# An attention backward kernel: dV and dK accumulated transposed, with 512 moving columns, and turned back on TensorE

## The chip, the cores and the metric

The kernel runs on one core of a Trainium2 chip. The metric is the device time of one execution in microseconds. Three runs of the kernel before gave 5147.52, 5152.12 and 5171.49 us, median 5152.12. Engines are called PE (TensorE: matmuls, and its weight loads PEld), DVE (VectorE), ACT (ScalarE), POOL (GpSimd) and SP (SyncE, which here issues transfers).

## The reference

Forward, with x of 2048 x 576 in bf16:

```
xn = layernorm(x)
s  = attention(xn @ wq, k_cache, v_cache) @ wo      # 32 heads, 2048 keys, 128 wide
g  = silu( (sigmoid(xn@w_gate) * (xn@w_up)) @ w_down )
out = x + s * g
```

The kernel returns `out` and the gradients with respect to x, both caches, wq, wo and the three weights of the gated block. For one head, with Q, K, V, dO of 2048 x 128, the attention part is

```
P  = softmax(Q K^T * 128**-0.5)      dV = P^T dO
dP = dO V^T                          dS = P * (dP - delta),  delta = rowsum(O * dO)
O  = P V                             dQ = dS K      dK = dS^T Q   (dQ, dK times the scale)
```

## The kernel before

Three stages surround each other: the gated block forward (to about 516 us), the 32 heads (to about 3767 us) and the weight gradients with dx (to the end). Only the heads are changed.

**Tiles of a head.** Queries go in 16 tiles of 128 rows (`qt`). For each, the scores of 2048 keys are made in two halves of 1024 columns (`s_half`: two matmuls of 512 moving columns into one of the two buffers of `ps_big`). DVE scales each half, takes the running minimum and writes `sneg`; ACT makes the exponential of the whole row (`s_exp`) into a slab `Pq` of 128 x 2048. P is left unnormalized; one over the row sum (`rinv`) is multiplied into dO's natural form `dOn` on POOL, two tiles at a time (`s_scale`), and into the outputs. In the same manner `dp_half` makes dP in two halves. The first half is usually moved out by ACT as `t` (minus delta) and multiplied by P on DVE; the second is one DVE instruction. The results are slabs `dSq`. There are 20 slabs for P and dS together.

**Two kinds of products.** The row passes (`row_mm`, L525) make O and dQ. They need P and dS transposed, which SP's transposing transfers give (`PT`, `dST`, one tile of dS by PE). Four query tiles share one accumulator bank. The column passes (`kv_mm`, L544) make dV and dK and use the slabs as they are: a block of 128 slab columns is the stationary operand, `dOn` or `Qn` of the same query tile moves with 128 columns, and the sum over the 16 query tiles stands in PSUM as [keys, 128]. A pass covers half of the keys, that is 8 blocks in two banks, 128 matmuls. When the last query tile is done, `sink` copies each bank to a staging tile `kv` (ACT) and POOL issues its output.

**The natural and transposed forms.** `prep_kt`, `prep_vt`, `prep_don` and `prep_qn` each turn eight 128 x 128 blocks on PE into one bank (`pt`, name `acct`), and one copy of 128 x 1024 moves it to SBUF. `proj` (L424, L425) makes Q^T and dO^T in four chunks of 512 columns.

**Banks.** `ps_acc` has four PSUM banks for everything but scores and dP: row accumulators, column accumulators (two per pass), projections and all transposes. `wt` has two buffers per tag; `t` is one tag.

**The order.** It is written out by hand. Every step gets a position with `at(pos, ...)`; a head has 64 positions (`HEAD`), S halves stand at 0 to 31 and dP halves at 32 to 63 (`anchor`), and the next head begins at 64, so that dK's passes and the last rows of dQ lie in the S half of the next head. The list is sorted by position and issued in that order, and under `manual_schedule` PE, DVE and ACT execute in this very order. In steady heads one position lasts about 1.57 us. SP's and POOL's instructions are ordered by a planner; they too run in order on their queues. The positions that matter here:

```
VA, VB, KA, KB = (22, 38.0), (38.5, 53.5), (58.0, 69.5), (70.5, 82.0)
QP, DO, KVE, PJE, OUE = (41.0, 3.0), (4.0, 2.5), "ss", "sv", "s"
KT_AT, DON_AT, VT_AT, QN_AT = (46.3, 2, "v"), (7.2, 5, "v"), (22.2, 2, "v"), (38.3, 2, "s")
EXP_AT, RINV_AT, PT_AT, DST_AT, AFTER = 2.1, 4.6, 2.7, 2.0, 3.5
```

VA and VB are start and end of dV's two passes (first and second half of the keys), KA and KB those of dK's; positions over 64 are in the next head (82 is its 18). The `_AT` triples are the position of the first group of eight blocks, the step to the second, and the engine of the copy, "v" DVE or "s" ACT. The exponential of tile qt stands at 2 qt + 2.1.

Of the kernel before, what the change touches and what calls it, by code (L numbers as in the profile page):

```python
# [9 lines left out]
bf = mybir.dt.bfloat16  # L10
f32 = mybir.dt.float32
PSUM = bass.MemoryType.PSUM
DRAM = bass.MemoryType.DRAM
P = 128
# [81 lines left out]
def kernel(  # L96
# [6 lines left out]
    nc = tc.nc  # L103
# [6 lines left out]
    NT = S // P  # L110
# [4 lines left out]
    CH = min(512, S)  # L115
# [32 lines left out]
    ident = pers.tile([P, P], bf, name="ident")  # L148
# [5 lines left out]
    alt = Alt(nc)  # L154
# [22 lines left out]
    with tc.tile_pool(name="pa", bufs=1) as pa:  # L177
        wd_sb = pa.tile([P, FT, D], bf, name="wd_sb")
        with tc.tile_pool(name="a1w", bufs=1) as wp:
# [11 lines left out]
            for bi in range(len(bounds) - 1):  # L191
                c0, c1 = bounds[bi], bounds[bi + 1]
# [72 lines left out]
        if True:  # L265
# [9 lines left out]
            with tc.tile_pool(name="a2h", bufs=1, reuse_waits="tile") as hp, \  # L275
# [12 lines left out]
                for sg in range(NT // SG):  # L288
# [7 lines left out]
                    for sl in range(SG):  # L296
# [7 lines left out]
                        for ft in range(FT):  # L304
                            for j, (n0, nn) in enumerate(ncs):
                                nc.tensor.matmul(accs[j][:, :nn], lhsT=hT_st[:, ft, :], rhs=wd_sb[:, ft, n0:n0 + nn],  # L306
                                                 start=(ft == 0), stop=(ft == FT - 1))
# [25 lines left out]
    KPC = CH // P  # L333
# [4 lines left out]
    with tc.tile_pool(name="ld2", bufs=2) as ld2, tc.tile_pool(name="ld1q", bufs=1) as ld1q, \  # L338
# [17 lines left out]
        def at(pos, fn, *args):  # L356
            prog.append((pos, len(prog), fn, args))

        def anchor(pos, fn, *args):
            anchors.append((pos, len(anchors), fn, args))  # L360
# [175 lines left out]
            if after:  # L536
                at(pos + step * (GQ - 1) + width + AFTER, after)

        def kv_mm(bx, hs, slabs, rhs, half, qt, j, sink):
            i, jj = j // KPC, j % KPC  # L540
            if qt == 0 and jj == 0:
                bx.acc[i] = ps_acc.tile([P, KPC, P], f32, name="acckv", tag="acc")
            k0 = (half * 2 * KPC + j) * P
            nc.tensor.matmul(bx.acc[i][:, jj, :], lhsT=slabs[qt][:, k0:k0 + P], rhs=getattr(hs, rhs)[:, qt, :],  # L544
                             start=(qt == 0 and jj == 0), stop=(qt == NT - 1 and jj == KPC - 1))
            if qt == NT - 1 and jj == KPC - 1:
                sink(bx.acc[i], i)

        def kv(pos, end, hs, slabs, rhs, half, out_dram):
            ov = out_dram.rearrange("(p t) d -> p t d", t=NT)  # L550
            bx = Box()
            bx.acc = [None, None]

            def sink(acc, i):
                c = half * 2 + i
                kv_t = stg.tile([P, KPC, P], bf, name="kv")
                alt.copy(kv_t[:], acc[:], eng=KVE[i])
                nc.gpsimd.dma_start(ov[:, c * KPC:(c + 1) * KPC, :], kv_t[:])

            n = 2 * KPC  # L560
            for qt in range(NT):
                for j in range(n):
                    at(pos + (end - pos) * (qt * n + j) / (NT * n), kv_mm, bx, hs, slabs, rhs, half, qt, j, sink)

        def o_sink(hs, g):
            gs = slice(g * GQ, (g + 1) * GQ)
# [28 lines left out]
        H1 = 2 * NT  # L595
        HEAD = 2 * H1
        XO, XQ = 12.1, 12.1
        VA, VB, KA, KB = (22, 38.0), (38.5, 53.5), (58.0, 69.5), (70.5, 82.0)
        QP, DO, KVE, PJE, OUE = (41.0, 3.0), (4.0, 2.5), "ss", "sv", "s"
        KT_AT, DON_AT, VT_AT, QN_AT = (46.3, 2, "v"), (7.2, 5, "v"), (22.2, 2, "v"), (38.3, 2, "s")  # L600
        EXP_AT, RINV_AT, PT_AT, DST_AT, AFTER = 2.1, 4.6, 2.7, 2.0, 3.5
        WO_AT = 50.0
        MAN = {mybir.EngineType.PE, mybir.EngineType.DVE, mybir.EngineType.Activation}
        for h in range(H):
            hs = Head(h)
            b = h * HEAD
            back = lambda x: b - HEAD + x if h else b - 14 + x / 8
            at(back(35.0), load_w, hs)
            at(back(35.1), load_kv, hs)
            for c in range(NCH):  # L610
                at(back(QP[0] + QP[1] * c), proj, hs, "QT", c, PJE[0])
                at(b + DO[0] + DO[1] * c, proj, hs, "dOT", c, PJE[1])
            at(b + DO[0] - 2, prep_wo, hs, "s")
            for g in range(2):
                at(back(KT_AT[0] + KT_AT[1] * g), prep_kt, hs, g, KT_AT[2])
                at(b + DON_AT[0] + DON_AT[1] * g, prep_don, hs, g, DON_AT[2])
                at(b + VT_AT[0] + VT_AT[1] * g, prep_vt, hs, g, VT_AT[2])
                at(b + QN_AT[0] + QN_AT[1] * g, prep_qn, hs, g, QN_AT[2])
            for p in range(NT // 2):
                at(b + 4 * p + 2 + RINV_AT, s_rinv, hs, p)  # L620
                at(b + max(4 * p + 2.1 + RINV_AT, DON_AT[0] + DON_AT[1] * (p // 4) + 0.5), s_scale, hs, p)
            for qt in range(NT):
                p1, p2 = b + 2 * qt, b + H1 + 2 * qt
                for hf in range(NHF):
                    anchor(p1 + hf, s_half, hs, qt, hf)
                    anchor(p2 + hf, dp_half, hs, qt, hf)
                at(p1 + EXP_AT, s_exp, hs, qt)
                if qt in PE_P:
                    for g in range(2):
                        at(p1 + 5.3 + g, trans_pe, hs.PT, hs.P, qt, "PT", g, "s")  # L630
                else:
                    at(p1 + PT_AT, trans_dma, hs.PT, hs.P, qt, "PT")
                if qt in PE_DS:
                    for g in range(2):
                        at(p2 + 4.3 + g, trans_pe, hs.dST, hs.dS, qt, "dST", g, "sv"[g])
                else:
                    at(p2 + DST_AT, trans_dma, hs.dST, hs.dS, qt, "dST")
            for g in range(NG):
                rows(b + 8 * g + XO, 2, 2, hs, hs.PT, "Vn", g, o_sink(hs, g))
                rows(b + H1 + 8 * g + XQ, 2, 2, hs, hs.dST, "Kn", g, dq_sink(hs, g))  # L640
            for half, (pv, pk_) in enumerate(((VA, KA), (VB, KB))):
                kv(b + pv[0], b + pv[1], hs, hs.P, "dOn", half, out_3[0, h])
                kv(b + pk_[0], b + pk_[1], hs, hs.dS, "Qn", half, out_2[0, h])
        bl = (H - 1) * HEAD
        assert WX + WD + 1 >= H
        for k, (h0, h1) in enumerate(((0, 8), (8, 16), (16, WX), (WX, WX + 7), (WX + 7, WX + WD))):
            if h0 < H - 1:
                at(bl + WO_AT + 3 * k, load_wo, h0, min(h1, H - 1))
        prog.sort(key=lambda e: e[:2])
# [10 lines left out]
    if True:  # L660
# [16 lines left out]
        with tc.tile_pool(name="c1b", bufs=1, side="right", reuse_waits="tile") as blk, \  # L677
# [32 lines left out]
            for st in range(NT):  # L710
# [12 lines left out]
                for h in range(H):  # L723
                    for j, (n0, nn) in enumerate(ncs):
                        nc.tensor.matmul(accs[j][:, :nn], lhsT=oT[:, h, :], rhs=wo_view(h)[:, n0:n0 + nn],
                                         start=(h == 0), stop=(h == H - 1))
# [17 lines left out]
        with tc.tile_pool(name="b1o", bufs=2, reuse_waits="tile") as outp, tc.tile_pool(name="b1t", bufs=3, reuse_waits="tile") as tmpp, \  # L744
# [21 lines left out]
            for fb in range(F // FB):  # L766
# [61 lines left out]
                for fl in range(FB // P):  # L828
                    frows = slice(fb * FB + fl * P, fb * FB + (fl + 1) * P)
                    accs = [ps.tile([P, 512], f32, name=f"accd{j}", tag="b") for j in range(len(ncs))]  # L830
                    for st in range(NT):
                        for j, (n0, nn) in enumerate(ncs):
                            nc.tensor.matmul(accs[j][:, :nn], lhsT=h_blk[:, st, fl * P:(fl + 1) * P], rhs=doB[:, st, n0:n0 + nn],  # L833
                                             start=(st == 0), stop=(st == NT - 1))
# [10 lines left out]
                for i in range(DL):  # L845
                    acc = ps.tile([P, 512], f32, name="accw", tag="b")
                    for st in range(NT):
                        nc.tensor.matmul(acc[:], lhsT=xn_all[:, st, i * P:(i + 1) * P], rhs=dd_blk[:, st, :, :],  # L848
                                         start=(st == 0), stop=(st == NT - 1))
                    alt.copy(stg_[:, i, :, :], acc[:].rearrange("p (k f) -> p k f", k=2))  # L850
                acc = ps.tile([P, 512], f32, name="accw", tag="b")
                for st in range(NT):
                    for k in range(2):
                        nc.tensor.matmul(acc[k * KL:(k + 1) * KL, :FB], lhsT=xn_all[:, st, DL * P:], rhs=dd_blk[:, st, k, :],
                                         start=(st == 0), stop=(st == NT - 1))
# [13 lines left out]
        with tc.tile_pool(name="c2b", bufs=1, reuse_waits="tile") as blk, tc.tile_pool(name="c2s", bufs=2, reuse_waits="tile") as sb, \  # L869
# [25 lines left out]
            for hg in range(NHG):  # L895
                cols = slice(hg * HG * P, (hg + 1) * HG * P)
                onb, dqb = held.pop(hg)
                for hl in range(HG):
                    h = hg * HG + hl
                    accs = [ps.tile([P, 512], f32, name=f"acc{j}") for j in range(len(ncs))]  # L900
                    for st in range(NT):
                        for j, (n0, nn) in enumerate(ncs):
                            nc.tensor.matmul(accs[j][:, :nn], lhsT=onb[:, st, hl * P:(hl + 1) * P], rhs=ds_all[:, st, n0:n0 + nn],  # L903
                                             start=(st == 0), stop=(st == NT - 1))
# [30 lines left out]
        with tc.tile_pool(name="c4c", bufs=1, reuse_waits="tile") as chp, tc.tile_pool(name="c4s", bufs=2, reuse_waits="tile") as sb, \  # L935
# [10 lines left out]
            for sbi in range(S // SB2):  # L946
# [7 lines left out]
                for pi, (src_d, wT, k0, KC, nm) in enumerate(passes):  # L954
# [5 lines left out]
                    for kk, sl in ([(kk, sl) for sl in range(nsl) for kk in range(KC)] if last else  # L960
# [3 lines left out]
                        for j, (n0, nn) in enumerate(ncs):  # L964
                            nc.tensor.matmul(accs[sl][j][:, :nn], lhsT=ch[:, kk, sl * P:(sl + 1) * P], rhs=w_[:, n0:n0 + nn],  # L965
                                             start=(pi == 0 and kk == 0), stop=(last and kk == KC - 1))
                for sl in range(nsl):
# [17 lines left out]
                    t = sb.tile([P, D], f32, name="t")  # L985
# [38 lines left out]
```

## Time and profile before

| | |
|---|---|
| median of three runs | 5152.12 us |
| profiled execution, its own time | 5157.5 us |
| its span | 5155.7 us |
| first exponential of head 0, last dQ copy of head 31 | 512.8, 3767.7 us |
| granted TensorE clock | 0.994 of full over the span, 1.00 in the heads |
| PE, DVE, ACT, POOL busy over the span | 97%, 63%, 44%, 27% |
| the same in head 20 (2530.60 to 2630.90 us) | 98.05, 84.53, 59.56, 32.73 of 100.30 us |
| a sneg half on DVE (L467) | 1.28 or 1.22 us |
| an exponential on ACT (L476) | 2.00 us |
| a copy of one bank, 512 f32 columns: ACT, DVE | 0.587, 0.689 us |
| a copy of one bank, 1024 bf16 columns: ACT, DVE | 1.018, 0.690 us |
| an output of dV or dK (L558): x256, issue on POOL, to landing | 0.553, 5.2 us |

A line of the groups names the line of the program, the engine, the operation, out<-in with buffer numbers left out, the shapes, the count, busy time and mean duration, and then the idle time before these instructions and what ended it. A line of the timeline has start, length, engine, line and operation; neighbours of one kind are merged, with their count, and in brackets stands an idle time before and what released it. Matmuls are pipelined, so the length of one is not what a further one costs: that is read from the distance of starts. A matmul of 128 moving columns is written 128x128, one of 512 columns 128x512.

### The profile page before, as it was taken

Reading aid. Unit: us, or ns where it says so; the run is one execution under the profiler, and the core shown is the slowest. Engines: PE = TensorE matmul, PEld = TensorE weight load, DVE = VectorE, ACT = ScalarE, POOL = GpSimd, SP = SyncE. Lnnn points to the kernel's source line nnn. Section 1 sums busy time; section 2 is a strip of 40 time slices with the busy share of each in tenths; the row PEclk is TensorE's granted clock in tenths of the full one; section 3 lists DMA queues with packets and bytes.
Section 4 is the critical chain, followed back from the end, with each engine's and each line's share of the span. In section 5 each row is a group of like instructions: output and inputs, shape, how many; then the busy total and the mean of one; then the engine's idle time right before and its main releaser. Section 6 shows DMA issues by size and latency. Waiting matters only on the chain.

```text
span 5155.7 us, 124622 instructions
## 1 busy us (share of the span) xinstructions
PE 4983.8 (97%) x53232; PEld 3490.9 (68%) x54160; DVE 3231.5 (63%) x5070; ACT 2285.3 (44%) x2878; POOL 1388.1 (27%) x1981
## 2 busy tenths in 40 slices
PE   8999999999999999999999999999899999999999
PEld 3444777777777777777777777777655555554554
DVE  5545888888888888888888888888733222210101
ACT  6531665566556556655655665566501222100000
POOL 2222333233223323332332333233222222111000
PEclk9999999999999999999999999999999999999999
DMA  7478999999999999999999999999999776697775
GB/s 281 184 210 166 189 191 196 195 199 195 196 196 196 197 201 199 196 202 196 199 196 198 199 197 195 199 199 195 205 200 246 209 209 196 199 246 166 158 153 118
DMA packets 2710509, 1013.89 MB, mean 197 GB/s; under 512 B 2523360, under 2 KB 2643936, under 8 KB 2709952
## 3 DMA queue, kind: packets, MB, share of 16 engines
q1 hardware_dynamic: 2628256, 726.57, 81.9%
q0 software_dynamic: 81696, 279.29, 18.5%
q8 instruction: 423, 6.93, 0.5%
q14 instruction: 134, 1.10, 0.1%
HBM read 172.54 MB, written 201.00 MB: 72 GB/s over the span
## 4 chain that ended last, share of the span: by engine, by line
PE 84%; DVE 6%; DMA 5%; issue 4%; SPq 1%; ACT 0%; DVEq 0%; ACTq 0%; another core or an unknown queue 0%
PE acckv L544 17%; PE acc L525 14%; PE acc L965 8%; PE dp L495 6%; PE sp L465 5%; DVE sneg L467 5%; PE accp L424 5%; PE accw L848 5%; DMA dST<-dSq 3%; PE g_ps L249 3%; PE u_ps L252 3%; PE accd L833 3%; PE acc L306 3%; PE acc L903 2%; PE dh L782 2%
## 5 line engine op out<-in xcount | busy, mean ns | idle before, releaser
L476 ACT ACTIVATE Pq<-sneg,nm 128x2048 bf16<-128x2048 bf16 x512 | 1024.5, 2001 | 389.5 <-DVE sneg L467 386.4
L525 PE MATMUL acc<-Kn,dST 128*128 128x128 bf16 x8192 | 1066.6, 219 | 28.1 <-DMA dST<-dSq 26.1
L544 PE MATMUL acckv<-dOn,Pq 128*128 128x128 bf16 x8192 | 1032.1, 219 | 15.4 <-POOL negdelta L579 0.2
L525 PE MATMUL acc<-Vn,PT 128*128 128x128 bf16 x8192 | 1023.2, 219 | 10.9 <-DMA PT<-Pq 9.1
L498 DVE SCALAR_TENSOR_TENSOR dSq<-dp,delta,Pq 128x1024 bf16<-128x1024 f32 x608 | 773.9, 1281 | 351.6 <-PE dp L495 249.7
L544 PE MATMUL acckv<-Qn,dSq 128*128 128x128 bf16 x8192 | 897.7, 220 | 8.4 <-issue 0.2
L544 PEld LDWEIGHTS <-Pq 128*128 128x128 bf16 x8192 | 793.8, 98 | 117.6 <-issue 0.9
L525 PEld LDWEIGHTS <-dST 128*128 128x128 bf16 x8192 | 758.8, 98 | 162.9 <-DMA dST<-dSq 34.1
L525 PEld LDWEIGHTS <-PT 128*128 128x128 bf16 x8192 | 766.4, 98 | 151.2 <-DMA PT<-Pq 11.3
L544 PEld LDWEIGHTS <-dSq 128*128 128x128 bf16 x8192 | 719.7, 98 | 99.8 <-issue 0.3
L467 DVE TENSOR_SCALAR_CACHE_REDUCE sneg<-sp,nm 128x1024 bf16<-128x1024 f32 x512 | 656.5, 1282 | 83.8 <-PE sp L465 46.4
L467 DVE TENSOR_SCALAR_CACHE_REDUCE sneg<-sp 128x1024 bf16<-128x1024 f32 x512 | 625.1, 1221 | 60.4 <-PE sp L465 42.0
L501 ACT ACTIVATE t<-dp,negdelta 128x1024 bf16<-128x1024 f32 x416 | 463.6, 1114 | 425.7 <-PE acc L525 233.2
L465 PE MATMUL sp<-KT,QT 128*128 128x512 bf16 x1763 | 548.4, 380 | 33.0 <-DVE sneg L467 26.1
L495 PE MATMUL dp<-VT,dOT 128*128 128x512 bf16 x1728 | 540.4, 379 | 0.8 <-DVE dSq L498 0.8
L484 POOL TENSOR_TENSOR dOn<-dOn,rinv_all 128x256 bf16<-128x256 bf16 x256 | 155.9, 609 | 657.7 <-DVE rinv_all L480 540.6
L505 DVE TENSOR_TENSOR dSq<-t,Pq 128x1024 bf16<-128x1024 bf16 x416 | 319.5, 768 | 0.0
L848 PE MATMUL accw<-dd_blk,xn_all 128*128 128x512 bf16 x1134 | 250.6, 379 | 0.9
L978 DVE SCALAR_TENSOR_TENSOR junk<-dxn,xn_all 128x576 f32<-128x576 f32 x16 | 12.1, 758 | 368.2 <-ACT dxn L973 368.2
L965 PEld LDWEIGHTS <-cf 128*128 128x128 bf16 x2304 | 145.7, 98 | 142.7 <-DMA cf<-dg_d 4.5
L591 POOL DMA_DIRECT2D dq_d<-dq_n x128 | 98.7, 771 | 459.5 <-DVE dq_n L590 450.9
L848 PEld LDWEIGHTS <-xn_all 128*128 128x128 bf16 x1152 | 111.4, 98 | 133.8
(182 smaller groups left out, 6694.3 us busy)
## 6 DMA issues: line engine op xcount, KB each, us to landing
out_dram<-kv POOLq DMA_DIRECT2D x256, 128.0 KB, 5.2
h_d<-h_row POOLq DMA_DIRECT2D x48, 384.0 KB, 2.7
a_d<-a_row POOLq DMA_DIRECT2D x48, 384.0 KB, 2.6
b_d<-b_row POOLq DMA_DIRECT2D x48, 384.0 KB, 3.2
a_blk<-a_d SPq DMA_DIRECT2D x18, 1024.0 KB, 5.6
b_blk<-b_d SPq DMA_DIRECT2D x18, 1024.0 KB, 20.8
du_d<-dd_blk POOLq DMA_DIRECT2D x18, 1024.0 KB, 8.5
dg_d<-dd_blk POOLq DMA_DIRECT2D x18, 1024.0 KB, 11.5
```

The source lines that it names most:

```text
L424: nc.tensor.matmul(acc[:], lhsT=w[:, i, :], rhs=srcT[:, i, cs], start=(i == 0), stop=False)
L465: nc.tensor.matmul(sp[:, c * CH:(c + 1) * CH], lhsT=hs.QT[:, qs], rhs=hs.KT[:, hf * HW_ + c * CH: hf * HW_ + (c + 1) * CH], start=True, st ...
L467: nc.vector.tensor_scalar(sneg[:, hf * HW_:(hf + 1) * HW_], sp[:], -SCALE, None if hf == 0 else nm[:, hf - 1:hf], op0=ALU.mult, op1=ALU.mi ...
L476: nc.scalar.activation(Pq[:], sneg[:], AF.Exp, bias=nm[:, hf:hf + 1], scale=-1.0, accum_out=hs.rs_all[:, qt:qt + 1])
L495: nc.tensor.matmul(dp[:, c * CH:(c + 1) * CH], lhsT=hs.dOT[:, qs], rhs=hs.VT[:, hf * HW_ + c * CH: hf * HW_ + (c + 1) * CH], start=True, s ...
L498: nc.vector.scalar_tensor_tensor(dSq[:, hsl], dp[:], hs.delta[:, qt:qt + 1], Pq[:, hsl], op0=ALU.subtract, op1=ALU.mult)
L501: nc.scalar.activation(t[:], dp[:], AF.Identity, bias=hs.negdelta[:, qt:qt + 1], scale=1.0)
L505: nc.vector.tensor_tensor(dSq[:, hsl], t[:], Pq[:, hsl], op=ALU.mult)
L525: nc.tensor.matmul(bx.acc[:, j, :], lhsT=T[qt][:, kt, :], rhs=getattr(hs, rhs)[:, kt, :], start=(kt == 0), stop=(kt == NT - 1))
L544: nc.tensor.matmul(bx.acc[i][:, jj, :], lhsT=slabs[qt][:, k0:k0 + P], rhs=getattr(hs, rhs)[:, qt, :], start=(qt == 0 and jj == 0), stop=(q ...
L848: nc.tensor.matmul(acc[:], lhsT=xn_all[:, st, i * P:(i + 1) * P], rhs=dd_blk[:, st, :, :], start=(st == 0), stop=(st == NT - 1))
L965: nc.tensor.matmul(accs[sl][j][:, :nn], lhsT=ch[:, kk, sl * P:(sl + 1) * P], rhs=w_[:, n0:n0 + nn], start=(pi == 0 and kk == 0), stop=(las ...
```

## The change

In the column passes the two operands change places: `dOn` or `Qn` of the query tile is now stationary, and 512 columns of the slab move. A pass is 32 matmuls instead of 128, into the same two banks, and its sum stands transposed, [128, keys]. At the end ACT copies each bank to a bf16 tile `kvT` (it shares the tag `t`), and a new step `kv_back`, one position after the pass's end, turns its eight blocks on PE into one more bank of `ps_acc`; DVE copies that to a staging tile `kv` (now one buffer of 128 x 1024), and POOL issues one output per pass instead of two. The passes get other positions. V^T's copies go from DVE to ACT and its second group from 24.2 to 26.6 (the first from 22.2 to 22.6). The third of dO^T's four chunks is copied by ACT. The second group of dO's natural form moves from 12.2 to 13.2.

```
+        def kv_mm(bx, hs, slabs, rhs, half, qt, i):
+            if qt == 0:
+                bx.acc[i] = ps_acc.tile([P, CH], f32, name="acckv", tag="acc")
+            c0 = (half * 2 + i) * CH
+            nc.tensor.matmul(bx.acc[i][:], lhsT=getattr(hs, rhs)[:, qt, :], rhs=slabs[qt][:, c0:c0 + CH],
+                             start=(qt == 0), stop=(qt == NT - 1))
+            if qt == NT - 1:
+                if i == 0:
+                    bx.T = wt.tile([P, 2, CH], bf, name="kvT", tag="t")
+                alt.copy(bx.T[:, i, :], bx.acc[i][:], eng=KVE[0])
+
+        def kv_back(bx, half, ov):
+            pt = ps_acc.tile([P, 8, P], bf, name="acct", tag="acc")
+            for j in range(2 * KPC):
+                nc.tensor.transpose(pt[:, j, :], bx.T[:, j // KPC, j % KPC * P:(j % KPC + 1) * P], ident[:])
+            kv_t = stg.tile([P, 2 * KPC, P], bf, name="kv", bufs=1)
+            alt.copy(kv_t[:], pt[:], eng=KVE[1])
+            nc.gpsimd.dma_start(ov[:, half * 2 * KPC:(half + 1) * 2 * KPC, :], kv_t[:])
...
             for qt in range(NT):
-                for j in range(n):
-                    at(pos + (end - pos) * (qt * n + j) / (NT * n), kv_mm, bx, hs, slabs, rhs, half, qt, j, sink)
+                for i in range(2):
+                    at(pos + (end - pos) * (qt * 2 + i) / (NT * 2), kv_mm, bx, hs, slabs, rhs, half, qt, i)
+            at(end + KV_BACK, kv_back, bx, half, ov)
...
-        VA, VB, KA, KB = (22, 38.0), (38.5, 53.5), (58.0, 69.5), (70.5, 82.0)
-        QP, DO, KVE, PJE, OUE = (41.0, 3.0), (4.0, 2.5), "ss", "sv", "s"
-        KT_AT, DON_AT, VT_AT, QN_AT = (46.3, 2, "v"), (7.2, 5, "v"), (22.2, 2, "v"), (38.3, 2, "s")
+        VA, VB, KA, KB = (21.3, 37.4), (37.9, 54.0), (59.5, 70.6), (71.1, 84.9)
+        QP, DO, KVE, PJE, OUE = (41.0, 3.0), (4.0, 2.5), "sv", ("ssss", "vvsv"), "s"
+        KT_AT, DON_AT, VT_AT, QN_AT = (46.3, 2, "v"), (7.2, 6, "v"), (22.6, 4, "s"), (38.3, 2, "s")
...
+        KV_BACK = 1.0
...
-                at(back(QP[0] + QP[1] * c), proj, hs, "QT", c, PJE[0])
-                at(b + DO[0] + DO[1] * c, proj, hs, "dOT", c, PJE[1])
+                at(back(QP[0] + QP[1] * c), proj, hs, "QT", c, PJE[0][c])
+                at(b + DO[0] + DO[1] * c, proj, hs, "dOT", c, PJE[1][c])
```

More of the change, by code (lines that the diff above doesn't have):

```diff
@@ L537, in rows @@
                 at(pos + step * (GQ - 1) + width + AFTER, after)
[L539 to L547, printed above, removed]
+        def kv_mm(bx, hs, slabs, rhs, half, qt, i):
[15 more added lines that the diff above has]
+            nc.gpsimd.dma_start(ov[:, half * 2 * KPC:(half + 1) * 2 * KPC, :], kv_t[:])
         def kv(pos, end, hs, slabs, rhs, half, out_dram):
@@ L552, in kv @@
             bx.acc = [None, None]
[L554 to L560, printed above, removed]
             for qt in range(NT):
-                for j in range(n):
-                    at(pos + (end - pos) * (qt * n + j) / (NT * n), kv_mm, bx, hs, slabs, rhs, half, qt, j, sink)
+                for i in range(2):
+                    at(pos + (end - pos) * (qt * 2 + i) / (NT * 2), kv_mm, bx, hs, slabs, rhs, half, qt, i)
+            at(end + KV_BACK, kv_back, bx, half, ov)
         def o_sink(hs, g):
```

## The prediction

> **What bounds the kernel now.** I read the page first, then PE's timeline inside one head, then the waits and the timelines of ScalarE (ACT) and VectorE (DVE) at the places that the edit touches. The page:
>
> ```profile
> span 5155.7 us, 124622 instructions
> PE 4983.8 (97%) x53232; PEld 3490.9 (68%) x54160; DVE 3231.5 (63%) x5070; ACT 2285.3 (44%) x2878; POOL 1388.1 (27%) x1981
> L544 PE MATMUL acckv<-dOn,Pq 128*128 128x128 bf16 x8192 | 1032.1, 219 | 15.4 <-POOL negdelta L579 0.2
> L544 PE MATMUL acckv<-Qn,dSq 128*128 128x128 bf16 x8192 | 897.7, 220 | 8.4 <-issue 0.2
> L431 PE MATMUL acct<-ident,Kn 128*128 128x128 bf16 x512 | 39.5, 220 | 0.0
> ```
>
> The chain of work that ended last is 84% PE. The heads run from 516 to 3767 us; the first exponentials of heads 20 and 21 start at 2530.61 and 2630.93, and 100.3 us is the commonest distance. The mean of 219 ns is a pipelined length, so starts must be read, in PE's timeline:
>
> ```profile
> 2001.70 0.61 PE L431 MATMUL acct<-ident,Kn 128*128 128x128 bf16 x8
> 2002.14 0.22 PE L544 MATMUL acckv<-dOn,Pq 128*128 128x128 bf16 x1
> ...
> 2004.63 1.03 PE L424 MATMUL accp<-xnT,wq_h 128*128 128x512 bf16 x4
> 2005.49 0.38 PE L425 MATMUL accp<-xnT,wq_h 128*128 128x512 bf16 x1
> ```
>
> Eight transposes take 0.44 us, four 512-column matmuls 0.86: 0.0558 us for 128 columns, 0.2157 for 512 (means over many starts). A head has 1024 matmuls of 128 columns in rows and kv passes, 85 transposes, and 168 matmuls of 512 columns: 57.1 + 4.7 + 36.2 = 98.1 us of the 100.3. PE is the bound, and some 2.3 us a head are stalls. Two kinds, again by starts:
>
> ```profile
> 2549.20 0.61 PE L431 MATMUL acct<-ident,dOT 128*128 128x128 bf16 x8 [0.22 <-DVE dq_n L590]
> ...
> 2560.44 0.61 PE L525 MATMUL acc<-Vn,PT 128*128 128x128 bf16 x8
> 2561.43 0.38 PE L465 MATMUL sp<-KT,QT 128*128 128x512 bf16 x1 [0.38 <-DVE sneg L467]
> ```
>
> The first is 0.39 us by starts. The second is 0.99 - 8 x 0.056 = 0.54, and three more like it (0.25, 0.27, 0.45) lie from 2559 to 2571: 1.52 us in all, where DVE's sneg releases the score banks late. The rest (0.16 before a QT projection, 0.09 elsewhere) I leave as it is.
>
> **The change, part by part.** Per head:
>
> PE stream. Out go 512 matmuls of 128 columns (28.6 us), in come 128 of 512 (27.6): -0.96. In come 32 transposes: 32 x 0.0558 = +1.79. Net +0.83, all on the path.
> The row says 0.055 us for one transpose in a stream. The Trainium skill, TensorE: Matmul & The Clock Gate, "Part 4: PE-mode transpose", gives about 275 ns in a kernel's context; by it the 32 would cost an estimated 8.8 us a head. The trace disagrees, 0.44 us for eight, and I go by the trace.
>
> S half, positions 16 to 32. Before, PE has 20.6 us of stream there and DVE 8 x 2.56 (a pair of snegs) + 2 x 0.69 (V^T) + 2 x 0.68 (delta) + 4 x 0.16 = 23.9. Of the 3.3 difference 1.52 shows as stall. After, V^T's copies go to ACT, one turn-back copy comes (0.69), and PE has 22.5 because dK's second pass now reaches to 20.9 and dV starts at 21.3: difference 0.7. I take the 1.52 as gone (-1.4 with a rest of 0.1); ends -1.52 and 0.
> dO natural, second group, one position later: its bank (released by dq_n) is free then. -0.39; ends -0.39 and 0.
>
> Four turn-backs. Each needs a bank of the four in ps_acc, both bf16 copies of its pass on ACT, and a DVE copy behind it. The row pass holds one bank, the next kv pass takes two, so there is one bank left. That is the new wait, and PE's queue stands behind it.
>
> dK first half, position 7.6. Live then: row, the next pass's two, and the bank of dO natural's first group. The turn-back must wait for that group's copy:
>
> ```profile
> 2538.73 1.28 DVE L467 TENSOR_SCALAR_CACHE_REDUCE sneg<-sp,nm 128x1024 bf16<-128x1024 f32 x1 [0.17 <-PE sp L465]
> 2539.94 0.69 DVE L42 COPY dOn<-acct 128x1024 bf16<-128x1024 bf16 x1
> ```
>
> Its transposes start at 2538.69, its copy ends 2540.63: 1.94. Between the two starts PE has only 0.88 us of work (8 transposes, 4 row matmuls, one kv matmul). Stall 1.1, with a semaphore and a slightly later sneg 1.2. Ends 0 and 1.4.
>
> dK second half, position 21.9. The last matmul of its first column block is at 20.04, of its second at 20.47, and the exponential of tile 9 at 20.10: ACT is in order, so the second copy runs behind the exponential. Before, both copies came ahead of one:
>
> ```profile
> 2557.80 1.07 ACT L40 CAST kv<-acckv 128x512 bf16<-128x512 f32 x2 [0.22 <-ACT Pq L476]
> 2558.76 2.02 ACT L476 ACTIVATE Pq<-sneg,nm 128x2048 bf16<-128x2048 bf16 x1
> ...
> 2560.75 0.58 ACT L40 CAST ou<-acc 128x512 bf16<-128x512 f32 x1
> 2561.41 2.00 ACT L476 ACTIVATE Pq<-sneg,nm 128x2048 bf16<-128x2048 bf16 x1
> ```
>
> From the end of the first block's matmul: 0.2 + 0.59 + 2.0 + 0.59 = 3.4 us until the second copy is done. PE has 1.9 us of work until the turn-back: stall 1.5. It could be 0.5 if the exponential could start before the first copy, 1.7 if its sneg is late.
>
> dV first half, position 38.4. Around it lie Q natural's first group (38.3), the next pass's first bank (37.9) and its second (38.403): four claims on three banks. The second must wait for the turn-back's own bank: 0.45 transposes + 0.2 + 0.69 copy on DVE against 0.45 on PE: 0.95. If it is handed Q natural's bank instead, whose ACT copy runs behind t of tile 3 (t now shares its two buffers with the new kvT tile and waits for the DVE product of tile 2), 2.2. Low end 0.
>
> ```profile
> 2584.81 1.07 ACT L40 CAST kv<-acckv 128x512 bf16<-128x512 f32 x2 [0.49 <-PE acckv L544]
> 2585.77 1.13 ACT L501 ACTIVATE t<-dp,negdelta 128x1024 bf16<-128x1024 f32 x1
> 2586.78 1.02 ACT L40 COPY Qn<-acct 128x1024 bf16<-128x1024 bf16 x1
> ```
>
> dV second half, position 55: both copies end about 1.2 us ahead, banks are free. 0; ends 0 and 0.7 (one DVE copy).
>
> Small things. dV's pass meets tile 14 at 35.4 instead of 36; POOL's scale of dO^ ends at 2581.85 and PE would come at about 2581.7: 0.1 (0 to 0.3). ACT gains 2 x 1.02 + 0.59 on 60 us of 100, DVE net +0.7 on 85: both hidden by PE except at the waits named; uncovered, DVE's would be the 0.7. One dO^T copy on ACT ends ahead of the next exponential: 0. POOL loses 4 of 8 output issues (0.55 each), off the path. The single staging buffer needs its 5.2 us landing, and turn-backs lie 13 or more positions (20 us) apart: 0. SP's transposes of P wait for exponentials that come 0.4 to 1.4 us later, and the row pass uses them 9 positions later: 0 while that holds. PE's waits on transposed tiles (26.1 + 9.1 us in the whole run) may shrink or grow: plus or minus 10 us in all, taken as 0.
>
> The sum. PE +0.83 x 32 = 27. dK stalls (1.2 + 1.5) x 31 = 84 (the last head's lie outside a next head). dV stalls (0.95 + 0.1) x 32 = 34. Stalls gone (1.4 + 0.39) x 31 = -55. Net +90 us. The profiled execution took 5157.5 us (span 5155.7), so 5247 for one like it; it stands 5.4 above the median of 5152.1, and against the median I forecast 5242, 1.7% slower.
>
> **The rivals.**
> *The turn-backs wait little, and the balanced S half wins (faster).* The gain of 1.9 us of stalls stands against 0.83 of stream. It decides when the four turn-backs together cost under about 1.1 us a head. With none: 27 - 59 = -32, 5120. For it: DVE's late sneg is a real wait in every head, and the moved pass fills just that stretch. Against it: ACT's order puts a 2.0 us exponential between the two copies, and three of four turn-backs come when no bank is free.
> *Half the waits.* If banks or copies come free earlier than my queues say, some 2 us of stalls a head: 27 + 60 - 55 = +32, 5184 (5126 to 5212).
> *The dV bank goes wrong.* The second bank of dV's second pass waits for Q natural's copy: 1.25 more a head, +40: 5282 (up to 5310).
> *The transposes do not stream.* If each of the 32 cost its whole row of 0.219 us, 32 x 0.163 = 5.2 us a head more, +167: 5409. The eight in 0.44 us speak against it. The skill's page named above points this way.
> *No change at all in the column passes*, because weight loads were hidden already: that is in the sum, which gives them only 0.96 us.
>
> **How the numbers follow.** Forecast (5212 to 5275) 0.57; dV bank 0.13; half the waits 0.16, of which 0.09 ends below 5178; faster 0.13; transposes 0.01. Range 5165 to 5300: it leaves out the faster case, the transposes and a few hundredths at the edges. A measurement of this kernel can tell about 0.5% (26 us) from no change, 5126 to 5178. Faster 0.13, same 0.09, slower 0.78.
>
> **What would show it.** Right: kv matmuls of 128x512, 128 a head, starts 0.216 apart; turn-back transposes in 0.45 us a group; PE idle before the turn-backs of dK, released by the dO natural copy on DVE and by ACT's kvT copy, and before the first matmul of dV's second pass; sneg waits gone; head distance near 103 us. Wrong: head distance under 101, or idle before the turn-backs under 0.3 us each; or kvT copies ahead of the exponentials on ACT; or PE stalled mainly on transposed tiles from the DMA queues.

## The result, and the profile after

The changed kernel is slower by about 1.5%. On one chip its median was 5238.25 us (five runs, 5234.73 to 5246.66) and that of the kernel before 5166.27 us; the ratio is 1.0152, with a 95% interval of 1.0129 to 1.0176. The profiled execution took 5246.66 us with a span of 5244.9, 89.2 us over the span before. All of it lies in the heads, as far as one execution of each tells: from the first exponential of head 0 to the last dQ copy the kernel before needs 3254.9 us, the changed one 3344.1. A steady head is now 104.05 us long; it was 100.32.

The page of the changed kernel, engines first, then the groups that answer to the ones shown of before:

```profile
span 5244.9 us, 102147 instructions
PE 5011.4 (96%) x42123; PEld 3031.1 (58%) x42896; DVE 3238.4 (62%) x5102; ACT 2354.9 (45%) x2974; POOL 1315.7 (25%) x1853
L543 PE MATMUL acckv<-dSq,Qn 128*128 128x512 bf16 x1921 | 718.0, 380 | 1.7
L543 PE MATMUL acckv<-Pq,dOn 128*128 128x512 bf16 x1826 | 693.1, 380 | 25.1 <-DVE kv L42 25.0
```

PE executes fewer instructions and its weight loads are busy 460 us less, yet the heads are longer. The loads were almost hidden already: four matmuls of 128 columns, each with its own load, took 4 x 0.0558 = 0.223 us by starts, and one of 512 with a single load takes 0.216. (A full count of the new matmuls is 2048 in each group; some records are missing.) What is new is who PE waits for. The longest waits of PE in the kernel before, as engine, line, what it waited for, us in total, times, longest:

```profile
PE acc L525 <- DMA dST<-dSq: 26.1, 24, 6.5
PE sp L465 <- DVE sneg L467: 26.1, 72, 1.0
PE acc L525 <- DMA PT<-Pq: 9.1, 6, 3.6
```

In the changed kernel:

```profile
PE acct L553 <- ACT kvT L40: 39.6, 31, 1.3
PE acct L553 <- DVE dOn L42: 25.4, 31, 0.8
PE acckv L543 <- DVE kv L42: 25.0, 32, 0.8
PE acc L525 <- ACT VT L40: 17.8, 31, 0.7
PE acc L525 <- POOL dOn L484: 9.1, 31, 0.3
PE dp L495 <- DVE dSq L498: 8.6, 32, 0.3
PE acc L525 <- DMA dST<-dSq: 8.4, 4, 4.6
PE sp L465 <- DVE sneg L467: 7.9, 12, 1.8
```

Six waits occur once in every head (31 or 32 times). The first two and the third are the ones forecast at the turn-backs; the fourth was not forecast. The sneg waits, 26.1 us in 72 places before, are down to 7.9 in 12, all of them at the start of head 0 (from 514 to 543 us). The waits on dS tiles from the transfers fell from 26.1 to 8.4.

PE's timeline shows the three turn-backs in head 20. The first three lines are dK's first half, the next two its second, the last two dV's first:

```profile
2599.96 0.22 PE L525 MATMUL acc<-Kn,dST 128*128 128x128 bf16 x1
2600.99 0.61 PE L553 MATMUL acct<-ident,kvT 128*128 128x128 bf16 x8 [0.82 <-DVE dOn L42]
2601.44 0.55 PE L525 MATMUL acc<-Kn,dST 128*128 128x128 bf16 x3
...
2623.38 0.22 PE L525 MATMUL acc<-Vn,PT 128*128 128x128 bf16 x1
2624.87 0.61 PE L553 MATMUL acct<-ident,kvT 128*128 128x128 bf16 x8 [1.28 <-ACT kvT L40]
...
2649.04 0.61 PE L553 MATMUL acct<-ident,kvT 128*128 128x128 bf16 x8
2650.43 0.38 PE L543 MATMUL acckv<-Pq,dOn 128*128 128x512 bf16 x1 [0.78 <-DVE kv L42]
```

By starts, with the stream taken off, these are 0.98, 1.44 and 0.945 us. The eight transposes themselves take 0.45 (2600.99 to 2601.44). The cause of the second stands in ACT's timeline of the changed kernel:

```profile
2621.77 0.58 ACT L40 CAST kvT<-acckv 128x512 bf16<-128x512 f32 x1
2622.25 2.00 ACT L476 ACTIVATE Pq<-sneg,nm 128x2048 bf16<-128x2048 bf16 x1
2624.16 0.19 ACT L476 ACTIVATION_READ_ACCUMULATOR Pq<-sneg,nm 128x1 f32 x1
2624.25 0.57 ACT L40 CAST kvT<-acckv 128x512 bf16<-128x512 f32 x1
```

One copy, a 2.00 us exponential, then the other copy, which ends at 2624.82; the transposes start at 2624.87. And the wait that I had not seen, at position 28, where the third row group asks for a bank, in PE's timeline and then in ACT's:

```profile
2634.14 0.59 PE L465 MATMUL sp<-KT,QT 128*128 128x512 bf16 x2
2635.30 0.27 PE L525 MATMUL acc<-Vn,PT 128*128 128x128 bf16 x2 [0.57 <-ACT VT L40]
```

```profile
2634.26 0.99 ACT L40 COPY VT<-acct 128x1024 bf16<-128x1024 bf16 x1
```

The second group of V^T was turned at 26.6 and its copy runs behind the exponential of tile 12, from 2634.26 to 2635.25. By the program all four banks are taken until then: 0.73 us by starts.

Another wait that was not forecast stands behind the turn-back of dV's second half, where DVE has one copy more:

```profile
2681.70 0.61 PE L525 MATMUL acc<-Kn,dST 128*128 128x128 bf16 x8
2682.58 0.59 PE L495 MATMUL dp<-VT,dOT 128*128 128x512 bf16 x2 [0.27 <-DVE dSq L498]
```

By starts it is 0.88 - 8 x 0.056 = 0.43; with 0.12 before another dP half just ahead of it, dP's waits are 0.55 us a head, where the kernel before has 0.09. (Two of the expectations below put them at 0.34, which is too little.)

### The profile page after: what moved, and what is told of

The parts are those of the page before. It is cut to its first block, busy times and chain, and to the rows that moved or that the text cites. A ratio compares the mean times of both kernels' runs of the same rounds, so it can differ in the third digit from the quotient of the medians.

```text
span 5244.9 us, 102147 instructions
## 1 busy us (share of the span) xinstructions
PE 5011.4 (96%) x42123; PEld 3031.1 (58%) x42896; DVE 3238.4 (62%) x5102; ACT 2354.9 (45%) x2974; POOL 1315.7 (25%) x1853
## 3 DMA queue, kind: packets, MB, share of 16 engines
q1 hardware_dynamic: 2628256, 726.57, 77.7%
## 4 chain that ended last, share of the span: by engine, by line
PE 78%; DVE 7%; issue 6%; ACT 4%; DMA 2%; POOL 1%; SPq 1%; DVEq 0%; POOLq 0%; ACTq 0%
PE acc L525 15%; PE acckv L543 13%; PE acc L968 7%; PE dp L495 7%; PE sp L465 6%; PE accw L851 4%; PE accp L424 4%; DVE sneg L467 3%; PE accd L836 3%; PE acc L306 3%; ACT Pq L476 3%; PE acc L906 2%; PE acc L728 2%; PE dh L785 2%; PE accq L916 2%
## 5 line engine op out<-in xcount | busy, mean ns | idle before, releaser
L525 PE MATMUL acc<-Kn,dST 128*128 128x128 bf16 x8192 | 947.4, 219 | 20.2 <-DMA dST<-dSq 8.4
L525 PEld LDWEIGHTS <-PT 128*128 128x128 bf16 x8192 | 686.5, 98 | 453.4 <-issue 63.8
L525 PEld LDWEIGHTS <-dST 128*128 128x128 bf16 x8192 | 675.0, 98 | 386.6 <-DMA dST<-dSq 10.4
L543 PE MATMUL acckv<-dSq,Qn 128*128 128x512 bf16 x1921 | 718.0, 380 | 1.7
L543 PE MATMUL acckv<-Pq,dOn 128*128 128x512 bf16 x1826 | 693.1, 380 | 25.1 <-DVE kv L42 25.0
L495 PE MATMUL dp<-VT,dOT 128*128 128x512 bf16 x1980 | 594.2, 379 | 8.7 <-DVE dSq L498 8.6
L505 DVE TENSOR_TENSOR dSq<-t,Pq 128x1024 bf16<-128x1024 bf16 x416 | 296.0, 712 | 0.0
L543 PEld LDWEIGHTS <-Qn 128*128 128x128 bf16 x2048 | 200.5, 98 | 53.4
L495 PEld LDWEIGHTS <-dOT 128*128 128x128 bf16 x2048 | 165.3, 98 | 109.4 <-issue 12.5
L543 PEld LDWEIGHTS <-dOn 128*128 128x128 bf16 x2048 | 200.5, 98 | 7.6 <-POOL dOn L484 7.6
L249 PE MATMUL g_ps<-wg_sb,xnT 128*128 128x512 bf16 x693 | 182.8, 388 | 12.3 <-DMA wg_sb<-in_B_w_gate_dram 6.0
```

The lines of the kernel that those rows point to most:

```text
L495: nc.tensor.matmul(dp[:, c * CH:(c + 1) * CH], lhsT=hs.dOT[:, qs], rhs=hs.VT[:, hf * HW_ + c * CH: hf * HW_ + (c + 1) * CH], start=True, s ...
L505: nc.vector.tensor_tensor(dSq[:, hsl], t[:], Pq[:, hsl], op=ALU.mult)
L525: nc.tensor.matmul(bx.acc[:, j, :], lhsT=T[qt][:, kt, :], rhs=getattr(hs, rhs)[:, kt, :], start=(kt == 0), stop=(kt == NT - 1))
L543: nc.tensor.matmul(bx.acc[i][:], lhsT=getattr(hs, rhs)[:, qt, :], rhs=slabs[qt][:, c0:c0 + CH], start=(qt == 0), stop=(qt == NT - 1))
```

## The experiments

The quantity compared is the distance between the first exponentials of neighbouring heads. Where the transfers do not interfere it repeats within 0.01 us, so one execution tells a few tenths. "Commonest" is its median over the last 30 distances, "mean" their average, "smallest" the least of them. In the kernel before the median is 100.46, but half of the distances stand together at 100.31 to 100.35; 100.32 is what I call its steady head. Medians of the kernel before moved from 5165 to 5178 us between chips, so totals are compared by ratios with runs on the same chip. The stages outside the heads took 1901 to 1928 us, depending on the execution, so the total of a single execution says little. Wherever a theory below names a total outright, the measured one came out higher, by 14 to 62 us.

### The turn-back left out

```
         def kv_back(bx, half, ov):
-            pt = ps_acc.tile([P, 8, P], bf, name="acct", tag="acc")
-            for j in range(2 * KPC):
-                nc.tensor.transpose(pt[:, j, :], bx.T[:, j // KPC, j % KPC * P:(j % KPC + 1) * P], ident[:])
             kv_t = stg.tile([P, 2 * KPC, P], bf, name="kv", bufs=1)
-            alt.copy(kv_t[:], pt[:], eng=KVE[1])
+            alt.copy(kv_t[:], bx.T[:].rearrange("p i (j d) -> p (i j) d", d=P), eng=KVE[1])
```

> Leaves out the eight transposes of every turn-back and the bank they need; DVE copies kvT to the staging tile as it stands, so dV and dK come out transposed. All else is the changed kernel, whose heads are 104.05 us apart. Theory (the loss is the stream of the transposes plus PE's waits at the turn-backs): 1.79 us of transposes and the waits 0.98 (dO natural's copy), 1.44 (exponential between the kvT copies) and 0.95 (bank of the turn-back) go, 5.16 us in all: heads 98.9 to 99.5 us apart (the upper end if DVE's copy, which still stands behind kvT, makes sneg late), total 5070 to 5095 us. Rival (another engine or the transfers set the pace, and waits come back as others): heads not under 102 us, total over 5170.

Measured: commonest distance 99.74, 4.31 us less than with the turn-back; one execution took 5131.0 beside a median of 5178.4 before. So the turn-backs, transposes and waits together, cost over 4 us of a 104 us head, and the rival is out. The distance is 0.24 over the range and the time 36 us: the wait on V^T's copy grew from 0.73 to 0.89 us, and two came, V^T's first group on the kvT copies (0.51) and dP on ACT's `t` (0.69).

### Three single waits in the changed kernel

Each edit changes one position, aimed at one wait.

dK's second pass ends earlier, so that both its copies precede the exponential of tile 9: `KB = (71.1, 84.0)` in place of `(71.1, 84.9)`.

> The changed kernel with dK's second pass ending at 84.0 instead of 84.9, so that both kvT copies stand ahead of the exponential of tile 9 on ACT, and its turn-back at 85.0. Theory: only PE's wait before that turn-back goes, 1.44 us a head: heads 102.6 us apart, total about 5193 us. Rival (DVE is the bound in the S half, and the wait returns before the score matmuls): heads 103.5 to 104.05 us apart, with sneg as the releaser of PE's waits.

Measured: 103.04, a gain of 1.01, where 1.44 was expected. PE's waits:

```profile
PE acct L553 <- DVE dOn L42: 25.4, 31, 0.8
PE acckv L543 <- DVE kv L42: 25.0, 32, 0.8
PE acc L525 <- ACT VT L40: 17.7, 31, 0.7
...
PE acct L431 <- DVE kv L42: 11.3, 31, 0.4
```

The line with kvT as releaser (39.6) is gone, which settles its cause; about a third of the 1.44 came back as a wait of V^T's first group on the turn-back's DVE copy (0.53 by starts), whose bank it needs. It did not return as sneg.

The turn-back of dK's first half comes later: `KV_BACK` 3.7 for that pass in place of 1.0.

> The changed kernel with the turn-back of dK's first half 3.7 positions after its pass instead of 1.0 (10.3 instead of 7.6), when the bank of dO natural has long been copied. Theory: PE's wait on DVE's copy of dO natural goes, 0.98 us a head: heads 103.05 us apart, total about 5207 us. It could go wrong by a wait on the bank of the third dO^T chunk, whose ACT copy ends close by: up to 0.5 us back. Rival (the wait returns elsewhere in the S half): heads 103.8 to 104.05.

Measured: 103.08 against 103.05 expected; the line with dO natural's copy is gone.

V^T's second group earlier: `VT_AT = (22.6, 2.4, "s")` in place of `(22.6, 4, "s")`.

> The changed kernel with V^T's second group at 25.0 instead of 26.6, so that its ACT copy stands ahead of the exponential of tile 12. Theory: PE's wait of 0.73 us a head in which the row pass has no bank until that copy goes: heads 103.3 us apart (104.05 before it), total about 5215 us. It may leave a part if the second group itself waits for the first group's copy: up to 0.5 back. Rival (the bank is held by something else): 104.0.

Measured: 103.33 against 103.3; the line with VT is gone.

### Q natural earlier, for dV's wait

`QN_AT = (34.8, 1.6, "s")` in place of `(38.3, 2, "s")`.

> The changed kernel with Q natural's groups at 34.8 and 36.4 instead of 38.3 and 40.3, so that at 38.4 three banks are free for three claims. Theory: PE's wait of 0.945 us before the first matmul of dV's second pass goes: heads 103.1 us apart, total about 5208 us. POOL then scales Q natural (1.9 us twice) beside delta's product, which may make dV's wait on POOL's scale of dO longer than 0.24: up to 0.5 back. Rival (another claim takes the bank): 103.8 to 104.05.

Measured: 103.90, not 103.1, which is inside the rival's band. The wait on the turn-back's bank did go, but the pass's first bank and the turn-back itself now wait for the kvT copies:

```profile
PE acckv L543 <- ACT kvT L40: 18.4, 32, 0.6
```

By starts that is 0.75 + 0.27 + 0.05 us a head. For the 0.75, ACT and DVE in head 20:

```profile
2649.05 0.58 ACT L40 CAST kvT<-acckv 128x512 bf16<-128x512 f32 x1 [0.91 <-DVE dSq L505]
```

```profile
2646.86 2.10 DVE L505 TENSOR_TENSOR dSq<-t,Pq 128x1024 bf16<-128x1024 bf16 x1
```

The first kvT copy does not stand in a queue: ACT is idle 0.91 us before it, until DVE's product releases it. By the program that product is the last reader of the `t` whose buffer kvT takes. And the product takes 2.10 us instead of 0.68, while POOL scales Q natural (2646.51 to 2648.41). The turn-back's 0.27 is a queue again: Q natural's second copy (1.02 us) runs between the two kvT copies. My expectation counted banks, and not what the copies that free them wait for. A tag of kvT's own, so that it shares no buffer with `t`, was not tried.

### The four edits together

KB as above, turn-back as above, `VT_AT = (23.2, 2.2, "s")`, `QN_AT = (34.8, 1.6, "s")`.

> The changed kernel with the four edits together (dK's second pass ends at 84.0; turn-back of its first half 3.7 positions after the pass; V^T's groups at 23.2 and 25.4; Q natural's at 34.8 and 36.4). Theory: of the waits only those of dP on DVE (0.34), of dV on POOL (0.23) and small ones stay on 98.97 us of stream: heads 99.6 to 100.2 us apart, total 5105 to 5140 us, under the kernel before. Rival (waits return as sneg waits or waits on the transposing transfers): heads 101 or more, or many heads above their median; total 5160 or more.

Measured: commonest distance 100.66, 3.39 less than the changed kernel, and 5156.6 us; the ratio to the kernel before is 0.9954 (0.9938 to 0.9970), so this version beats both. Of the 3.73 us by which a steady head had grown, 3.39 were a matter of places. It misses the range by 0.46 and the total by 17 us. What is left is the dV boundary again (0.67 + 0.27 + 0.05 us by starts, with the same DVE product of 2.09 us ahead of the kvT copy) and dP's waits, 0.55 where the expectation has 0.34:

```profile
2579.00 0.55 PE L525 MATMUL acc<-Vn,PT 128*128 128x128 bf16 x7
2580.08 0.38 PE L543 MATMUL acckv<-Pq,dOn 128*128 128x512 bf16 x1 [0.53 <-ACT kvT L40]
```

### Two more placements of that boundary

The first puts the turn-back of dV's first half at 39.9 and Q natural's groups at 38.3 and 40.9 (the next head's Q^T chunks from 42.0). The second moves dV's first pass to end at 38.0 and the last turn-back to 57.0 as well.

> As the run with four edits, but Q natural's groups at 38.3 and 40.9, the next head's Q^T chunks from 42.0 in steps of 2.8 (they were from 41.0 in steps of 3.0), and the turn-back of dV's first half 2.5 positions after its pass (39.9), when Q natural's first bank has been copied; dV's second pass then has its two banks at once. Theory: the waits of 0.69, 0.27 and 0.05 us that the four edits left at dV's passes go: heads 99.6 to 99.9 us apart, about 30 us less in all than with the four edits, some 5125 us. Rival (with PE faster than the transposing transfers allow, waits on transposed tiles come instead): the commonest distance falls as said, but the mean over the heads stays over 100.3 us.

> The former run's kernel, with dV's first pass ending at 38.0 (second from 38.5), so that tile 14 meets POOL's scale later, its turn-back at 40.1, and the turn-back of dV's second half 3.0 after its pass (57.0), away from the two groups of dS that PE transposes. Theory: dV's wait on POOL's scale (0.23) and dP's on DVE (0.34) go for the most part: heads 99.1 to 99.5 us apart. Rival as for the former run: the mean over the heads stays over 100.3 us.

Measured: commonest 100.78 and 100.85, means 100.93 and 101.06, ratios 0.9980 (0.9964 to 0.9997) and 0.9973 (0.9950 to 0.9995). Both theories miss, by 0.9 and 1.35 us, and neither version is better than the former. The rival does not hold either, since the commonest distance did not fall. In the first, PE waits 0.79 us for Q natural's ACT copy before the turn-back; in the second the waits on POOL's scale and most of dP's (0.55 to 0.16) are gone as meant, and Q natural's second group waits 1.27 us for the turn-back's DVE copy instead. With four banks, that place keeps waits of about 0.9 to 1.3 us under every order that I tried.

### Only the new places, with the old passes

```
-        VA, VB, KA, KB = (22, 38.0), (38.5, 53.5), (58.0, 69.5), (70.5, 82.0)
-        QP, DO, KVE, PJE, OUE = (41.0, 3.0), (4.0, 2.5), "ss", "sv", "s"
-        KT_AT, DON_AT, VT_AT, QN_AT = (46.3, 2, "v"), (7.2, 5, "v"), (22.2, 2, "v"), (38.3, 2, "s")
+        VA, VB, KA, KB = (21.3, 37.4), (37.9, 54.0), (59.5, 70.6), (71.1, 84.9)
+        QP, DO, KVE, PJE, OUE = (41.0, 3.0), (4.0, 2.5), "ss", ("ssss", "vvsv"), "s"
+        KT_AT, DON_AT, VT_AT, QN_AT = (46.3, 2, "v"), (7.2, 6, "v"), (22.6, 4, "s"), (38.3, 2, "s")
```

> The kernel before (column passes of 128 moving columns, no turn-back) with only the changed kernel's places: passes, V^T copies on ACT, dO natural's second group, one dO^T chunk on ACT. Theory: the stream stays at 98.15 us; the sneg waits (1.52) and the wait on dq_n (0.39) go, the wait of the row pass on V^T's ACT copy (0.73) and of dV on POOL's scale (0.24) come: heads 99.3 to 99.6 us apart, total 5120 to 5140 us, the transfers' waits in some heads included. Rival (the places bring nothing by themselves, or the transfers allow no shorter head): heads at 100.3 us or over, total 5145 or more.

Measured: smallest distance 100.92, mean 101.82, ratio 1.0037 (1.0018 to 1.0056). The rival holds. The sneg waits did go, as expected, but the new ends of dK's passes hurt the old form too:

```profile
PE acc L525 <- DMA dST<-dSq: 33.2, 25, 6.6
PE acckv L544 <- ACT kv L40: 32.8, 62, 0.9
PE acc L525 <- ACT VT L40: 13.4, 30, 0.6
```

The second line is the copy behind an exponential: the next pass waits for the old pass's bank, 0.39 us after dK's first half and 0.99 after its second by starts. In this kernel an end of a pass just after an exponential costs PE whether or not something is turned back.

### V^T's copies on ACT, with the old passes and places

`VT_AT = (22.2, 2.8, "s")` and the second group of dO natural at 13.2, nothing else.

> The kernel before with its own passes and places, and only V^T's copies on ACT (groups at 22.2 and 25.0) and dO natural's second group at 13.2. It tests my reading of the waits of the kernel before: if V^T's DVE copies cause the sneg waits (1.52 us a head) and the early group the wait on dq_n (0.39), most of both go: heads 98.6 to 99.4 us apart, total 5115 to 5150 us with the transfers' waits. Rival (DVE is late in the S half without them too, or the transfers allow no shorter head): heads 100 or more.

Measured: smallest distance 99.48, mean 100.72; ratio 0.9980 (0.9958 to 1.0002), no difference that can be told. The smallest distance is 0.08 over the theory's range, the mean inside the rival's. The wait on dq_n is gone, and the last of the four sneg waits (0.45). The other three are there unchanged (0.25, 0.54, 0.27 by starts):

```profile
2562.01 0.61 PE L525 MATMUL acc<-Vn,PT 128*128 128x128 bf16 x8
2563.00 0.59 PE L465 MATMUL sp<-KT,QT 128*128 128x512 bf16 x2 [0.38 <-DVE sneg L467]
...
2564.74 0.61 PE L431 MATMUL acct<-ident,Vn 128*128 128x128 bf16 x8
```

They lie before V^T is turned at all, so V^T's copies can't be their cause. They lie where PE has only scores and one row pass between dK's end (18.0) and dV's start (22).

### That stretch closed, with the old passes

```
-        VA, VB, KA, KB = (22, 38.0), (38.5, 53.5), (58.0, 69.5), (70.5, 82.0)
+        VA, VB, KA, KB = (21.0, 38.0), (38.5, 53.5), (58.0, 69.5), (70.5, 84.0)
-        KT_AT, DON_AT, VT_AT, QN_AT = (46.3, 2, "v"), (7.2, 5, "v"), (22.2, 2, "v"), (38.3, 2, "s")
+        KT_AT, DON_AT, VT_AT, QN_AT = (46.3, 2, "v"), (7.2, 6, "v"), (22.6, 2.4, "s"), (38.3, 2, "s")
```

> The kernel before with its 128-column passes, no turn-back, and only the stretch without column passes closed: dK's second pass ends at 84.0 instead of 82.0 and dV's first starts at 21.0 instead of 22; V^T's copies on ACT at 22.6 and 25.0, dO natural's second group at 13.2. Theory: the sneg waits that stayed with V^T's copies on ACT (0.25, 0.54, 0.27) came from PE having only row passes and scores between 18 and 22, so that DVE sets the pace there; with the gap closed they go: commonest distance 98.4 to 98.8 us. If PE alone is the bound, the mean over the heads follows and the total is some 5105 to 5120 us. Rival (the transposing transfers allow no mean under about 100.3 us): the commonest distance falls, waits on transposed tiles take up the rest, mean 100.2 or more, total 5150 or more.

Measured: smallest distance 98.42, the shortest of all, and no sneg waits in steady heads, so the gap was the cause. And the time does not follow: mean 101.45, ratio 1.0011 (0.9992 to 1.0031). What the rival of this run says came true, in distance, waits and time; that its limit is 100.3 us is not shown. PE's waits:

```profile
PE acc L525 <- DMA dST<-dSq: 58.8, 51, 5.0
PE acc L525 <- DMA PT<-Pq: 35.0, 36, 3.7
```

93.8 us of waits on transposed tiles; the kernel before has 35.2.

### One transposing transfer less

```
-    PE_DS = {9}
+    PE_DS = {9, 13}
```

> The kernel with old passes and the gap closed (commonest stall-free distance 98.42 us, mean 101.5), and one more of a head's dS tiles (13) turned by PE instead of a transposing transfer: 30 such transfers a head instead of 31, 16 PE transposes (0.89 us) more. Theory: the transfers' engines are what the heads run into once PE has less than about 100.5 us: PE's waits on transposed tiles (58.8 + 35.0 us) fall by half or more, smallest distance 99.3, mean 99.6 to 100.6 us, total below that kernel by 30 to 55 us. Rival (those waits come from the order on the transfer queue or from late slabs, not from the load): they stay over 70 us, and the mean rises by the 0.9 us of PE work to about 102.

Measured: commonest distance 99.42, smallest 99.36, mean 100.08; 5130.7 us, ratio to the kernel before 0.9923 (0.9900 to 0.9946). Of the kernels that leave nothing out it has the lowest time and the lowest ratio. PE's waits:

```profile
PE acc L525 <- DMA dST<-dSq: 26.7, 23, 4.9
...
PE acc L525 <- DMA PT<-Pq: 7.7, 2, 7.5
```

From 93.8 to 34.4 us for one transfer in 31. A longer stream on PE alone would not do that: the mean fell by 1.37 us although PE works 0.9 us a head more. And the waits on P's tiles fell with the others, from 35.0 to 7.7, although no transfer of P was dropped. So the transfers are what the heads run into, and fewer of them help. That it is their load and nothing else is not shown: the edit also changes the order on the queue, and three versions with the same 31 transfers have means as far apart as 100.24 (the turn-back left out), 100.72 (V^T's copies on ACT) and 101.45 (the gap closed), which one fixed limit would not give. This run and the former were on different chips; the two ratios allow for that.

## Why the prediction was right

5242 us was forecast, 5238.25 measured. As a change that is 90 us forecast (1.7%) and 72 measured by the medians (1.5% by the ratio). The forecast starts from 5152.12, the median of three runs before, and the median of all five is 5166.27, so part of the nearness comes from the choice of runs. By steps, per head:

- Stream, +0.83: right. Starts of the new matmuls are 0.216 apart, eight transposes take 0.45. The about 275 ns a transpose of the Trainium skill (TensorE: Matmul & The Clock Gate, "Part 4: PE-mode transpose") are not what this kernel shows.
- dK's first half, 1.2 forecast: 0.98 measured, and the releaser is the named DVE copy; moving the turn-back removed 0.97.
- dK's second half, 1.5 forecast: 1.44, behind the exponential as argued; moving the pass's end removed it.
- dV's first half, 0.95 forecast: 0.945, on the turn-back's DVE copy. (The terms given for it, 0.45 + 0.2 + 0.69 - 0.45, add to 0.89, so the exact hit is chance.)
- dV's second half, 0 forecast: PE does not wait at the turn-back, but dP's waits a little later grew from 0.09 to 0.55. The upper end, 0.7, was for one DVE copy. Where this turn-back was moved to 57.0, among other edits, 0.16 was left, which speaks for that copy.
- POOL's scale, 0.1 forecast: 0.24.
- V^T's copies on ACT, "hidden by PE except at the waits named": wrong. 0.73 us a head, because the bank of the second group is held behind an exponential. The prediction follows ACT's queue at the four turn-backs alone, though every copy that frees a bank stands in it.
- Stalls that go, -1.4 and -0.39: right in size (1.52 and 0.39 are gone). But I gave V^T's copies as one reason together with the moved passes. The runs show the moved passes did it for three of the four; V^T's copies made only the last, 0.45.
- Transfers, "plus or minus 10 us in all, taken as 0": the mean distance before is 100.99 where the steady head is 100.32, after it is 104.05 for both. So 0.67 us a head of waits went, some 20 us in all, twice the stated end. Whether the longer head or the quicker transfers (last section) did it, the runs do not separate.

The forecast sum was 2.8 us a head, a distance of 103.1. The steady distance grew by 3.73, which the measured terms above add up to within 0.1, and the mean by 3.06. So waits that were missed (V^T 0.73, dP 0.46) and a relief that was missed (0.67) nearly cancel. The mechanism at the turn-backs and its places were right, but for dP behind the last one; the nearness of 4 us is luck in good part.

The faster rival named its own condition, turn-backs under about 1.1 us a head. They cost 3.4 in waits here. With the four edits together the waits at the dV boundary come to about 1, and that kernel is indeed 0.46% under the one before.

## What to carry to other kernels

A bank is free only when its copy has run, and the copy waits its turn in an in-order queue: before moving a pass, write down for each claim on a bank which copy frees it, what stands ahead of that copy, and who still reads the buffer that it writes. Here one 2 us exponential between two 0.6 us copies cost 1.4 us of the bounding engine in every head. Before shortening the bounding engine's work, look for the next bound: in this kernel PE could be brought to 98.4 us a head, and with the old passes nothing came of it until one transfer in 31 was taken off the transfers' queue.

## What was not expected of the hardware

A product on DVE slows down beside POOL's scale of Q natural. The product `dSq<-t,Pq` (L505, bf16 from bf16) takes at most 0.684 us wherever no tensor operation of POOL lies beside it (289 times in the kernel before). The 32 that overlap POOL's scale of Q natural (L455) take 1.77 to 1.83 us there, 1.07 in the changed kernel, where they overlap 0.53 us of it instead of 1.26, and up to 2.10 with Q natural earlier (1.54). Why is not shown.

The same transfers took less time beside the transposed passes. The page's line for the transposing and other hardware queue has the same packets and bytes in both kernels, before first, then after:

```profile
q1 hardware_dynamic: 2628256, 726.57, 81.9%
```

```profile
q1 hardware_dynamic: 2628256, 726.57, 77.7%
```

81.9% of 5155.7 us is 4223 us of packet time for each transfer engine, 77.7% of 5244.9 is 4075, 3.5% less. It holds for every version with the same transfers: the four with the old passes have 4186 to 4248 us, the nine with transposed passes 4075 to 4117. It is not only the longer head: the version with four edits, with heads about as long as before, has 79.5% of 5152.0, 4096 us. Why, the runs do not tell. The old passes read the slabs as stationary operands, with 512 weight loads a head where the new ones have 128, and they issue 256 outputs of dV and dK instead of 128; neither was tried alone. It suggests that the transposed form leaves the transfers more room, which would be a use of it beside PE's stream, and transposed passes with one transposing transfer less remain to be tried.
